# Sums of token blocks by accumulating transfers from GpSimd in an attention and feed-forward kernel

## The chip, the cores and the metric

The kernel runs on one core of one Trainium2 chip. The metric is the device time of that core in microseconds. A core has five engines, each with its own instruction queue that is worked off in order: TensorE (PE in the profile) for matrix products, VectorE (DVE), ScalarE (ACT), GpSimd (POOL) and SyncE (SP). Transfers between the chip's memory and the core's buffer are carried out by 16 DMA engines; an engine's queue only issues them. An engine stops at an instruction until everything that this instruction waits for has arrived, and all that stands behind it in the same queue stops too.

## The reference

```python
def _attn_ref(q, k, v):
    S = q.shape[2]
    scale = 1.0 / np.sqrt(q.shape[-1])
    scores = scale * np.matmul(q, k.transpose(0, 1, 3, 2)) - np.log(S)
    attn = 1.0 / (1.0 + np.exp(-scores))
    return np.matmul(attn, v)

def _moe_ref(x, w_in, w_out, s, b):
    h = x @ w_in
    r = np.maximum(h, 0.0)
    g = s * (r * r) + b
    return g @ w_out
```

q, k and v are 8 batches x 12 heads x 448 rows x 64 columns. The attention's output, laid out as 3584 tokens of 768 values, is the x of the second function; w_in is 768 x 2048 and w_out 2048 x 768. All is float32.

## The kernel before

There are two big parts. The first computes the attention, 24 pairs of head groups one after the other, and writes its output x to the chip's memory in eight pieces, one per batch (`x_dram`). Beside it VectorE and ScalarE turn the weights into the form that the second part needs.

The second part is the feed-forward network over seven blocks of 512 tokens (TB). Block 0 is done in the plain way (`ffn1`, `ffn2`). The other six are taken in two groups of three blocks, which the code calls `threes`. For a group, the 3 x 3 products of token blocks with weight blocks are not all formed: by a scheme in the manner of Strassen, 15 products of sums are formed instead, and the results are combined. Each factor is a signed sum of blocks of tokens or of weights. The sums of the weights are made once and lie in memory (`wd`); the sums of the tokens are made anew for each group, in the core's buffer. Each product is done in three matrix multiplications per tile, because every factor is split into a high and a low part (`split_hi` on ScalarE, `split_lo` on VectorE).

For each group there is a layer 1 (720 matmuls, line 1095) and a layer 2 (720 matmuls, line 1225). A layer is a loop over 60 units of 12 matmuls. `L1` gives the units' order: the 15 products in six chains, each chain for two of the four pieces p of the hidden layer at a time. The products of a chain add into the same accumulator tile (two banks of the PE's accumulators), and after each product of a chain a copy (ScalarE, `copy`, line 968) or a sum (VectorE, lines 178 and 181) takes the running sum out, before the next product of the chain may add to it. So in the chain (10, 13, 2) unit 8 is product 10 for p = 0, unit 9 product 10 for p = 1, and unit 10 is product 13 for p = 0, which goes into the tile of unit 8 and cannot begin before ScalarE has copied unit 8's result out.

The order around the change is written by hand. The nine blocks of a group, `a00` to `a22` (third of the tokens, third of the 768 columns), each 128 x 1024 float32 or 512 KB, are loaded by `load_raw`. `first_jobs(n)` makes for each of the 15 products a list of jobs: the sums of blocks that it needs (`new` for a sum into a new buffer, `into` for one into an old), then `hi` and `lo` of the split. The table `places` says after which unit u of layer 1 the next job of which product is put into the queues, and `early_jobs` does the same in layer 2 of the group before. So unit 7 has `(8,)`, and the job of product 8 that falls there is its `hi`. The job stands in ScalarE's queue ahead of the copy of unit 7's own result. Per group there are 15 sums of blocks, 30 in all, each one VectorE instruction of 128 x 1024 elements at line 178 or 181.

SyncE issues nearly all transfers: one weight fetch per unit (`wu<-wd`, line 663, 512 KB), which runs six units ahead of the PE through seven buffers; the loads of token blocks (line 337, one load in two pieces where it crosses from one batch to the next); the stores of results (line 838); and, in layer 1 of the first group only, loads and stores of `later_sums`, which makes the rest of the weight sums for layer 2 (lines 899, 902, 912). GpSimd has no work.

Of the kernel before, what the change touches and what calls it, by code (L numbers as in the profile page):

```python
# [18 lines left out]
ALU = mybir.AluOpType  # L19
# [17 lines left out]
TB = 512  # L37
# [57 lines left out]
def sigmoid_attention_relu2_ffn(  # L95
# [10 lines left out]
    nc = tc.nc  # L106
    B, NQ, P, _, _, S = qk.shape
    D = v.shape[5]
    NF, _, DM = w_in.shape
# [4 lines left out]
    KC = NCC // 3  # L114
# [8 lines left out]
    def pool(stack, name, bufs, side=None, space=None):  # L123
        kw = dict(side=side) if side else {}
        if space is not None:
            kw["space"] = space
        return stack.enter_context(
            tc.tile_pool(name=name, bufs=bufs, reuse_waits="tile", **kw)
        )
# [21 lines left out]
    heap = Slots(pool(ctx, "h0", 1), 1, "g")  # L151
# [14 lines left out]
    x_dram = [dram.tile([P, NCC, S], F32, name=f"xd_{b}") for b in range(B)]  # L166
# [59 lines left out]
    def op(o, x, sign, y):  # L226
        (add if sign > 0 else sub)(o, x, y)
# [103 lines left out]
    def load_tokens(dst, t, c0, n):  # L331

        at = t * TB
        while at < (t + 1) * TB:
            b = at // S
            m = min((t + 1) * TB, (b + 1) * S) - at
            nc.sync.dma_start(
                dst[:, :, at - t * TB : at - t * TB + m],
                x_dram[b][:, c0 : c0 + n, at - b * S : at - b * S + m],
            )  # L340
            at += m


    at = ExitStack()
# [250 lines left out]
    for n, (b, t) in enumerate(quads):  # L595
        if n:
            ticks(n, "DVE")
        a = scores(b, t, loaded[n])
# [52 lines left out]
    threes = [tuple(1 + 3 * n + i for i in range(3)) for n in range((NT - 1) // 3)]  # L651
# [14 lines left out]
    def slot(name, r=False):  # L666
        return heap.tile([P, 2, TB], F32R if r else F32, name=name)

    A = {}

    def load_raw(n, m, k):
        A[m, k] = slot(f"a_{n}_{m}{k}")
        load_tokens(A[m, k], threes[n][m], KC * k, KC)

    def split_hi(raw, sign, name):
        hi = slot(name + "h", True)
        if sign > 0:
            nc.scalar.copy(hi, raw)
        else:
            nc.scalar.activation(hi, raw, AF.Copy, scale=-1.0)  # L680
        return hi

    def split_lo(raw, sign, hi, name, own):

        lo = slot(name + "l", True)
        if sign > 0:
            sub(lo, raw, f32(hi))
        else:
            nc.vector.scalar_tensor_tensor(
                lo, raw, -1.0, f32(hi), op0=ALU.mult, op1=ALU.subtract  # L690
            )
        if own:
            heap.free(raw)
        return lo
# [3 lines left out]
    def first_jobs(n):  # L698

        jobs = {}  # L700

        def split(i, get, own=False):
            def hi():
                opd[i] = [split_hi(get(), FIRST[i][1], f"s{i}_{n}")]

            def lo():
                opd[i].append(split_lo(get(), FIRST[i][1], opd[i][0], f"s{i}_{n}", own))

            return [hi, lo]

        def a(m, k):
            return lambda: A[m, k]

        def new(key, x, y, sign=1):
            def job():
                A[key] = slot(f"a_{n}_{key}")
                op(A[key], A[x], sign, A[y])

            return job

        def into(x, y, z, sign=1, drop=()):


            def job():
                op(A[x], A[y], sign, A[z])
                for d in drop:
                    heap.free(A.pop(d))

            return job

        a00, a01, a02, a10, a11, a12, a20, a21, a22 = ((m, k) for m in range(3) for k in range(3))
        jobs[4] = split(4, a(*a00))
        jobs[3] = [new("3", a00, a20), into("3", "3", a21)] + split(3, lambda: A["3"], True)
        jobs[10] = [into(a22, a21, a22)] + split(10, a(*a22))
        jobs[13] = [new("13", a00, a22)] + split(13, lambda: A["13"], True)
        jobs[2] = [new("2", a02, a22)] + split(2, lambda: A["2"], True)
        jobs[1] = split(1, a(*a01))
        jobs[8] = [new("10", a11, a12), new("11", a01, "10")] + split(8, lambda: A["11"])
        jobs[12] = [into(a11, a10, a11), into(a11, a11, a01, 1, (a01,))] + split(12, a(*a11), True)
        jobs[7] = split(7, a(*a21))  # L740
        jobs[9] = [new("9", a10, a21, -1)] + split(9, lambda: A["9"], True)
        jobs[11] = [into(a12, a12, a21, -1, (a21,))] + split(11, a(*a12), True)
        jobs[5] = split(5, lambda: A["10"], True)
        jobs[0] = [into(a02, a02, "11", 1, ("11",)), into(a02, a02, a00, -1, (a00,))]
        jobs[0] += split(0, a(*a02), True)
        jobs[6] = split(6, a(*a10))
        jobs[14] = [into(a20, a20, a22, -1, (a22,)), into(a20, a10, a20, 1, (a10,))]
        jobs[14] += split(14, a(*a20), True)
        return jobs

# [23 lines left out]
    todo = first_jobs(0)  # L774
# [89 lines left out]
    def weights():  # L864
        fetch()
        return fetched[next(pos_)]


    places = {
# [4 lines left out]
    }  # L874
    LAST = ((0, slice(0, TB)), (1, slice(0, TB // 2)), (1, slice(TB // 2, TB)))
    LEAD = 3

# [73 lines left out]
    for n, blocks in enumerate(threes):  # L951
# [128 lines left out]
        for u, (i, p) in enumerate(L1):  # L1080
            wt = weights()
            if n == 0 and u < 4:
                load_raw(0, *start[5 + u])
            if outs and u > 4:
                out_store(outs[0], evict[6 - 2 * len(outs)], 0, 2)
                heap.free(outs.pop(0))
            ch = next(c for c in CHAINS_1 if i in c)
            if i == ch[0]:
                banks[p] = ps.tile([P, 2, TB], F32, tag="b", name=f"h_{n}_{i}_{p}")
            bk = banks[p]  # L1090
            for j in range(2):
                m = 0
                for c in range(KC):
                    for wi, xi in PARTS:
                        nc.tensor.matmul(  # L1095
                            bk[:, j], wt[:, j, wi, c * P : (c + 1) * P], opd[i][xi][:, c, :],
                            start=i == ch[0] and m == 0,
                            stop=m == 3 * KC - 1,
                            skip_group_check=True,
                        )  # L1100
                        m += 1
            if p == NPP - 1:
                for t in opd.pop(i):
                    heap.free(t)
                for key in {3: ("3",), 13: ("13",), 2: ("2",), 9: ("9",), 5: ("10",), 0: ((0, 2),),
                            12: ((1, 1),), 11: ((1, 2),), 14: ((2, 0),)}.get(i, ()):
                    A.pop(key)
            here = places.get(u, ())
            casts = []
            for q_ in (10,) * (n == 0 and u < 2) + here:  # L1110
                fn = todo[q_].pop(0)
                if u < 4 and fn.__name__ == "hi":
                    casts.append(fn)
                else:
                    fn()
            if u >= len(L1) - LEAD:
                prep(u - len(L1) + LEAD)
            ready, scales = scales, []
            for _ in range(2 - len(here)):
                if later:  # L1120
                    later.popleft()()
            results_1(i, p, bk)
            for fn in casts + ready:
                fn()
            for f, units in LATER_SUMS.items() if n == 0 else ():
                for _ in range(units.count(u)):
                    next(later_sums_[f], None)
# [10 lines left out]
        def results_2(i, bk):  # L1138
# [60 lines left out]
            elif n + 1 < len(threes):  # L1199
# [5 lines left out]
                heap.free(C.pop(4))  # L1205

        todo = first_jobs(n + 1) if n + 1 < len(threes) else {}
        loads = {38 + 2 * x: start[x] for x in range(9)} if todo else {}
        early_jobs = {50: (4,), 52: (4,), 53: (3,), 54: (3,), 55: (3,), 56: (3,), 57: (10,), 58: (10,), 59: (10,)}
        for j, (i, p) in enumerate(L2):  # L1210
            wt = weights()
            ch = next(c for c in CHAINS_2 if i in c)
# [5 lines left out]

            for e, tk in LAST if end else [(e, slice(TB)) for e in range(KC)]:
                o = bk[:, e]  # L1220
# [10 lines left out]
                if end:  # L1231
                    x = C["t"][:, e, tk]
# [57 lines left out]
```

## Time and profile before

| | |
|---|---|
| median of the runs | 1038.8 us (2 runs, 1038.2 to 1039.39) |
| span of the profiled execution, first to last instruction | 1037.5 us |
| layer 1, first group | 381.56 to 544.76 us |
| layer 2, first group | to 707.96 us |
| layer 1, second group | to 871.16 us |
| layer 2, second group | to the end |
| sums of token blocks | 1.22 us each on VectorE |

No time is given for the profiled execution as a whole; its span is 1.3 us below the median of the runs, and that is what lies around the span. The profile gives busy times per engine, a strip of 40 slices, the chain of work that ended last, groups of instructions by line and the DMA issues. The trace behind it gives each instruction's start, its length and what ended the wait ahead of it. In its rows `a<-a,a` is a sum of token blocks, `s_0h<-a` and `s_0l<-a` are the high and low part of a factor of the first group (`s_1h` of the second), `G<-h` is a copy of a result out of the accumulators, `wu<-wd` a weight fetch, and SPq is SyncE's queue as it issues transfers.

### The profile page before, as it was taken

What the parts mean: (1) busy time and instruction counts of PE and PEld (TensorE: products, weight loads), DVE (VectorE), ACT (ScalarE), POOL (GpSimd) and SP (SyncE); (2) the same over time, 40 slices, a digit from 0 to 9 for tenths busy, and PEclk for the clock granted to TensorE, in tenths of its full rate; (3) what the DMA queues carried; (4) which work ended last, traced back from release to release, by engine and by line L of the source; (5) the groups of instructions that cost most, each with busy time, mean ns of one, the idle gap of its engine ahead of it and who ended that gap; (6) DMA issues with size and microseconds to landing.
All of it is one profiled execution on the core that took longest, in us unless ns stands there. A gap on an engine that the chain in (4) does not pass through costs nothing.

```text
span 1037.5 us, 13898 instructions
## 1 busy us (share of the span) xinstructions
PE 1033.7 (100%) x5288; PEld 780.3 (75%) x5288; DVE 836.1 (81%) x906; ACT 617.2 (59%) x666; POOL 0.2 (0%) x4
## 2 busy tenths in 40 slices
PE   9999999999999999999999999999999999999998
PEld 4545555555888888888888888888888888888887
DVE  5999999995988965898898897796455789888777
ACT  7999999988776755564445344344445335552432
POOL 0000000000000000000000000000000000000000
PEclk9999999999999999999999999999999999999999
DMA  9788989995999999999686676897666666676773
GB/s 327 269 331 342 360 317 393 346 396 194 332 366 367 358 408 410 341 341 322 201 269 189 218 229 220 291 317 249 197 190 195 194 193 197 190 236 207 222 228 118
DMA packets 101568, 287.16 MB, mean 277 GB/s; under 512 B 10240, under 2 KB 20352, under 8 KB 101504
## 3 DMA queue, kind: packets, MB, share of 16 engines
q1 hardware_dynamic: 101216, 285.84, 79.6%
q8 instruction: 42, 0.69, 0.3%
q10 hardware_dynamic: 288, 0.46, 0.1%
q14 instruction: 22, 0.18, 0.0%
HBM read 198.18 MB, written 88.08 MB: 276 GB/s over the span
## 4 chain that ended last, share of the span: by engine, by line
PE 100%; DVE 0%; issue 0%
PE o L1225 31%; PE h L1095 31%; PE pav L454 11%; PE psc L420 9%; PE ph L563 6%; PE po L765 6%; PE psc_l L441 2%; PE pav L463 2%; PE psc L426 0%; PE idle L482 0%; DVE C_t L181 0%
## 5 line engine op out<-in xcount | busy, mean ns | idle before, releaser
L1095 PE MATMUL h<-s_1h,wu 128*128 128x512 f32 x480 | 148.0, 389 | 0.0
L1095 PE MATMUL h<-s_0h,wu 128*128 128x512 f32 x480 | 147.8, 389 | 0.0
L400 ACT ACTIVATE a<-psc,nls 128x896 f32<-128x896 f32 x144 | 132.7, 1008 | 12.9 <-PE psc L420 10.1
L454 PE MATMUL pav<-a,v 128*64 128x448 f32 x576 | 113.8, 543 | 0.0
L1095 PEld LDWEIGHTS h<-s_1h,wu 128*128 128x128 f32 x480 | 90.1, 188 | 18.8
L1095 PEld LDWEIGHTS h<-s_0h,wu 128*128 128x128 f32 x480 | 90.1, 188 | 18.6
L968 ACT COPY G<-h 128x1024 f32<-128x1024 f32 x48 | 48.8, 1017 | 85.5 <-PE h L1095 57.8
L860 ACT ACTIVATE G<-G,b_sb,s_sb 128x1024 f32<-128x1024 f32 x48 | 59.8, 1246 | 61.4 <-DVE G L857 60.7
L1095 PE MATMUL h<-s_0l,wu 128*128 128x512 f32 x240 | 93.4, 389 | 0.0
L1095 PE MATMUL h<-s_1l,wu 128*128 128x512 f32 x240 | 93.4, 389 | 0.0
L454 PEld LDWEIGHTS pav<-a,v 128*64 128x64 f32 x576 | 39.1, 137 | 63.8 <-issue 45.4
L178 DVE TENSOR_TENSOR G<-G,h 128x1024 f32<-128x1024 f32 x40 | 48.8, 1219 | 39.4 <-PE h L1095 39.3
L1225 PE MATMUL o<-g_3h,wu 128*128 128x512 f32 (+1 forms) x244 | 79.0, 385 | 0.0
L1225 PE MATMUL o<-g_0h,wu 128*128 128x512 f32 x240 | 78.8, 389 | 0.0
L1225 PE MATMUL o<-g_1h,wu 128*128 128x512 f32 x240 | 78.8, 389 | 0.0
L1225 PE MATMUL o<-g_2h,wu 128*128 128x512 f32 x240 | 78.8, 389 | 0.0
L765 PE MATMUL po<-g,w 128*128 128x512 f32 x288 | 67.7, 389 | 0.0
L765 PEld LDWEIGHTS po<-g,w 128*128 128x128 f32 x288 | 54.1, 188 | 11.2
L563 PE MATMUL ph<-x0h,w 128*128 128x512 f32 x192 | 61.7, 390 | 0.0
L420 PE MATMUL psc<-qkh 64*128 64x448 f32 x282 | 54.1, 380 | 0.0
L1225 PEld LDWEIGHTS o<-g_3h,wu 128*128 128x128 f32 x244 | 45.6, 188 | 9.2
L1095 PEld LDWEIGHTS h<-s_0l,wu 128*128 128x128 f32 x240 | 45.0, 188 | 9.4
(152 smaller groups left out, 2028.0 us busy)
## 6 DMA issues: line engine op xcount, KB each, us to landing
wu<-wd SPq DMA_DIRECT2D x240, 512.0 KB, 3.6
wd<-t SPq DMA_DIRECT2D x36, 768.0 KB, 8.6
qk<-qk_t SPq DMA_DIRECT2D x23, 896.0 KB, 7.4
st<-w_out SPq DMA_DIRECT2D x16, 768.0 KB, 10.3
st<-w_in SPq DMA_DIRECT2D x16, 768.0 KB, 9.3
wd<-w SPq DMA_DIRECT2D x16, 768.0 KB, 5.6
v<-v_t SPq DMA_DIRECT2D x24, 448.0 KB, 6.1
xd<-xo SPq DMA_DIRECT2D x24, 448.0 KB, 4.9
```

The lines of the kernel that those rows point to most:

```text
L178: nc.vector.tensor_tensor(o, x, y, op=ALU.add)
L400: nc.scalar.activation(a, psc[:, :, :S], AF.Sigmoid, bias=nls, scale=SCALE)
L420: nc.tensor.matmul(o[:, j, :S], two[wi][r, i, cols], two[xi][r, i, :S], start=m == 0, stop=m == 2,)
L441: nc.tensor.matmul(psc[half[i], j, :S], x[r, i, 1, 3 * P :], x[r, i, 0, :], start=True, stop=True,)
L454: nc.tensor.matmul(pav[r, i, :S], ld_[1][:, 3 * i + c, j, :], a[i, c][:, j, :], start=c == 0, stop=False,)
L463: nc.tensor.matmul(pav[r, i, :S], ld_[1][half[i], 6, j, :], a[half[i], j, :], start=False, stop=True,)
L563: nc.tensor.matmul(ph, w[:, k, wi, kc * P : (kc + 1) * P], x0[h][xi][:, cc, :], start=m == 0, stop=m == 3 * NCC - 1,)
L765: nc.tensor.matmul(pos[e], w[:, k, wi, kc * P : (kc + 1) * P], g[:, gi, :], start=first and i == 0, stop=last and i == 2,)
L860: nc.scalar.activation(x, x, AF.Identity, bias=b_sb, scale=s_sb)
L968: nc.scalar.copy(g(m, h), bk)
L1095: nc.tensor.matmul(bk[:, j], wt[:, j, wi, c * P : (c + 1) * P], opd[i][xi][:, c, :], start=i == ch[0] and m == 0, stop=m == 3 * KC - 1, sk ...
L1225: nc.tensor.matmul(o, wt[:, f, wi, e * P : (e + 1) * P], g[gi][:, f, tk], start=(end or i == ch[0] and p == 0) and f == 0 and m == 0, stop ...
```

## The change

Of the 30 sums, 14 are no longer made by VectorE. A new helper `plus` has GpSimd issue a transfer that adds its source to its destination. A sum into a new buffer becomes a plain load of one addend from `x_dram` into that buffer, issued by SyncE (`copy`), and then an accumulating transfer of the other addend (`plus_into`). A sum into an old buffer becomes the accumulating transfer alone. In each group six sums go this way (jobs `"s"`); in the second group the two sums of product 3 do too, the second of them straight from `x_dram` in two pieces (`plus_tokens`). These make 15 accumulating transfers. `SUMS_BY_DMA` places the six: two after unit 2, one each after units 4, 5, 9 and 41. The sums of product 3 in the second group are placed at step 47 of layer 2 of the first group, six steps ahead of where VectorE made them. The places of all `hi` and `lo` jobs stay as they were.

```diff
+    def plus(x, y):
+        nc.gpsimd.dma_start(out=x, in_=y, accum_op=ALU.add)
...
+        def copy(key, m, k):
+            A[key] = slot(f"a_{n}_{key}")
+            load_tokens(A[key], threes[n][m], KC * k, KC)
+
+        def plus_into(x, y, drop=()):
+            plus(A[x], A[y])
+            for d in drop:
+                heap.free(A.pop(d))
+
+        def eleven():
+            copy("11", 0, 1)
+            plus_into("11", "10")
+
+        def three():
+            copy("3", 0, 0)
+            plus_into("3", (2, 0))
+            plus_tokens(A["3"], threes[n][2], KC, KC)
+
+        def ten():
+            copy("10", 1, 1)
+            plus_into("10", (1, 2))
...
-        jobs[3] = [new("3", a00, a20), into("3", "3", a21)] + split(3, lambda: A["3"], True)
+        jobs[3] = [new("3", a00, a20), into("3", "3", a21)] if n == 0 else [three, lambda: None]
+        jobs[3] += split(3, lambda: A["3"], True)
...
-        jobs[8] = [new("10", a11, a12), new("11", a01, "10")] + split(8, lambda: A["11"])
-        jobs[12] = [into(a11, a10, a11), into(a11, a11, a01, 1, (a01,))] + split(12, a(*a11), True)
+        jobs["s"] = [
+            ten, eleven, lambda: plus_into(a11, a10), lambda: plus_into(a11, a01, (a01,)),
+            lambda: plus_into(a02, "11", ("11",)), lambda: plus_into(a20, a10, (a10,)),
+        ]
+        jobs[8] = split(8, lambda: A["11"])
+        jobs[12] = split(12, a(*a11), True)
...
-        jobs[0] = [into(a02, a02, "11", 1, ("11",)), into(a02, a02, a00, -1, (a00,))]
+        jobs[0] = [into(a02, a02, a00, -1, (a00,))]
...
-        jobs[14] = [into(a20, a20, a22, -1, (a22,)), into(a20, a10, a20, 1, (a10,))]
+        jobs[14] = [into(a20, a20, a22, -1, (a22,))]
...
+    SUMS_BY_DMA = {2: 2, 4: 1, 5: 1, 9: 1, 41: 1}
...
+            for _ in range(SUMS_BY_DMA.get(u, 0)):
+                todo["s"].pop(0)()
...
-        early_jobs = {50: (4,), 52: (4,), 53: (3,), 54: (3,), 55: (3,), 56: (3,), 57: (10,), 58: (10,), 59: (10,)}
+        early_jobs = {47: (3, 3), 50: (4,), 52: (4,), 55: (3,), 56: (3,), 57: (10,), 58: (10,), 59: (10,)}
```

The queues change at three places. The first is SyncE's queue around unit 2 of the first group. Before (`a_12` and `a_10` are token blocks, `wu_0_10_1` the weights of unit 9):

```order
L663 DMA wu_0_10_0_3855<-wd_0_91 128x1024
L337 DMA a_12_3857<-xd_85 128x2x320
L337 DMA a_12_3857<-xd_86 128x2x192
L663 DMA wu_0_10_1_3878<-wd_1_92 128x1024
L337 DMA a_10_3880<-xd_85 128x2x320
L337 DMA a_10_3880<-xd_86 128x2x192
L663 DMA wu_0_13_0_3901<-wd_0_91 128x1024
```

and in the changed kernel, where `a_10_3872` and `a_11_3876` are the new buffers "10" and "11":

```order
L337 DMA a_12_3857<-xd_85 128x2x320
L337 DMA a_12_3857<-xd_86 128x2x192
L337 DMA a_10_3872<-xd_85 128x2x320
L337 DMA a_10_3872<-xd_86 128x2x192
L337 DMA a_11_3876<-xd_84 128x2x384
L337 DMA a_11_3876<-xd_85 128x2x128
L663 DMA wu_0_10_1_3886<-wd_1_92 128x1024
L337 DMA a_10_3888<-xd_85 128x2x320
L337 DMA a_10_3888<-xd_86 128x2x192
L663 DMA wu_0_13_0_3909<-wd_0_91 128x1024
```

Four loads, together 1 MB, stand ahead of the weights of unit 9, of block `a_10` and of all that follows.

The second is GpSimd's queue, which issued nothing before. The six transfers of the first group:

```order
L672 DMA a_10_3872<-a_12_3857 128x1024
L672 DMA a_11_3876<-a_10_3872 128x1024
L672 DMA a_11_3831<-a_10_3888 128x1024
L672 DMA a_11_3831<-a_01_3807 128x1024
L672 DMA a_02_3632<-a_11_3876 128x1024
L672 DMA a_20_3551<-a_10_3888 128x1024
```

The second reads what the first writes and waits for it; the fourth adds to what the third has added to and waits for that.

The third is ScalarE's queue between units 5 and 11 of the first group, whose order is the same in both kernels. In the changed one:

```order
L1011 COPY G_003_3946<-h_4_3_3932 128x1024
L1011 COPY G_202_3963<-h_4_2_3911 128x1024
L693 CAST s_0h<-a_11_3876 128x1024
L1011 COPY G_203_3986<-h_4_3_3932 128x1024
L1011 COPY G_210_4005<-h_10_0_3990 128x1024
L1011 COPY G_211_4023<-h_10_1_4009 128x1024
```

The cast is the `hi` of product 8. Its source is now the buffer that the second accumulating transfer fills, and the copies of units 7, 8 and 9 stand behind it.

More of the change, by code (lines that the diff above doesn't have):

```diff
@@ L669, in sigmoid_attention_relu2_ffn, with plus_tokens @@
     A = {}
+    def plus(x, y):
+        nc.gpsimd.dma_start(out=x, in_=y, accum_op=ALU.add)
+    def plus_tokens(dst, t, c0, n):
+        at = t * TB
+        while at < (t + 1) * TB:
+            b = at // S
+            m = min((t + 1) * TB, (b + 1) * S) - at
+            plus(
+                dst[:, :, at - t * TB : at - t * TB + m],
+                x_dram[b][:, c0 : c0 + n, at - b * S : at - b * S + m],
+            )
+            at += m
     def load_raw(n, m, k):
```

8 rows, old and new, of the table places are left out of this document.

## The prediction

> **What bounds the kernel now.** I read the profile's first parts, then the chain of waits in order of time, and then the timelines of single queues at the places that the change touches. The page first:
>
> ```profile
> PE 1033.7 (100%) x5288; PEld 780.3 (75%) x5288; DVE 836.1 (81%) x906; ACT 617.2 (59%) x666; POOL 0.2 (0%) x4
> PEclk9999999999999999999999999999999999999999
> PE 100%; DVE 0%; issue 0%
> ```
>
> PE alone makes the chain that ends last. A busy PE in this profile need not be a PE at its pace, so the stages' lengths decide. The chain in order of time has the two groups as four pieces:
>
> ```profile
> 381.56 163.20 PE h L1095 x720
> 544.76 163.20 PE o L1225 x720
> 707.96 163.20 PE h L1095 x720
> 871.16 163.28 PE o L1225 x726
> ```
>
> All four last the same: 163.20 us / 720 = 226.7 ns per matmul, 2.72 us per unit of 12. Layer 1 of the first group, with all the extra work on VectorE and the DMA engines, is not a hundredth of a us longer than layer 1 of the second. So no matmul there waits for anything. VectorE, 81% busy, is always in time. What the change takes off VectorE can therefore gain nothing: it can only be hidden, or cost. A gain of 2% (20.8 us, about what a measurement of this kernel can tell from no change) would need fewer or faster matmuls, and the clock row is full already.
>
> **What is removed.** Fourteen sums of 1.22 us, by this group of VectorE's instructions (the larger of the two groups of such sums after 395 us):
>
> ```profile
> L178 DVE TENSOR_TENSOR a<-a,a 128x1024 f32<-128x1024 f32 x17 | 20.7, 1220 | 3.2 <-DMA a<-xd 3.1
> ```
>
> That is 14 x 1.22 = 17.1 us of VectorE's time, worth 0 by the above. The PE's work hides it, and nothing takes that cover away.
>
> **What is added.** On SyncE: five loads of 512 KB, ten issues. On GpSimd, whose queue is else empty: 15 transfers. The cost is not in issuing them. It is when a sum is ready, and who stands in a queue waiting for it. The place that has least room is product 8 of the first group. ScalarE's timeline there, before:
>
> ```profile
> 400.63 1.02 ACT L968 COPY G<-h 128x1024 f32<-128x1024 f32 x1 [1.71 <-PE h L1095]
> 401.54 1.05 ACT L678 CAST s_0h<-a 128x1024 fp32r<-128x1024 f32 x1
> 403.35 1.01 ACT L968 COPY G<-h 128x1024 f32<-128x1024 f32 x1 [0.76 <-PE h L1095]
> 406.07 1.01 ACT L968 COPY G<-h 128x1024 f32<-128x1024 f32 x1 [1.71 <-PE h L1095]
> 408.79 1.01 ACT L968 COPY G<-h 128x1024 f32<-128x1024 f32 x1 [1.71 <-PE h L1095]
> 411.75 1.06 ACT L680 ACTIVATE s_0h<-a 128x1024 fp32r<-128x1024 f32 x1 [1.42 <-DVE a L178]
> ```
>
> The copy at 400.63 is unit 6's, the cast at 401.54 is the `hi` of product 8, and the next three are the copies of units 7, 8 and 9. The PE itself needs product 8 only at unit 22, 40 us later. But the copies stand behind the cast. Unit 10 starts at 381.56 + 10 x 2.72 = 408.8 us and adds into the tile that unit 8's copy reads. From the row starts, cast and two copies take 0.95 + 0.91 + 1.01 us, with some 0.2 us to hand on: about 3.1 us. So the cast may start as late as 408.8 - 3.1 = 405.7 us, and every us beyond that stops the PE.
>
> When is the sum "11" ready? VectorE's two sums started here, held until block `a12` had landed:
>
> ```profile
> 398.81 2.49 DVE L178 TENSOR_TENSOR a<-a,a 128x1024 f32<-128x1024 f32 x2 [3.08 <-DMA a<-xd]
> ```
>
> SyncE had issued that block's two loads from 390.77 on:
>
> ```profile
> 388.94 0.33 SPq L663 DMA_DIRECT2D wu<-wd  x1
> 390.77 1.59 SPq L337 DMA_DIRECT2D a<-xd  x2
> 393.03 0.33 SPq L663 DMA_DIRECT2D wu<-wd  x1
> 393.41 1.58 SPq L337 DMA_DIRECT2D a<-xd  x2
> 395.50 0.86 SPq L663 DMA_DIRECT2D wu<-wd  x2
> 398.11 0.32 SPq L663 DMA_DIRECT2D wu<-wd  x1
> ```
>
> In the changed kernel the load for "10" comes right behind `a12`. The stretch is full of transfers:
>
> ```profile
> 392.00:403.00 11.00, 11.00 (x50) 9.09 (x50) 5.03 (x5) 5.99 (x6) 0.00 (x0) 1.00 1.05 405
> 403.00:414.00 11.00, 11.00 (x50) 9.13 (x49) 6.06 (x7) 5.56 (x6) 0.00 (x0) 1.00 1.03 415
> 414.00:425.00 11.00, 11.00 (x50) 9.09 (x49) 10.36 (x15) 6.11 (x8) 0.00 (x0) 1.00 0.82 297
> ```
>
> (last two columns: DMA share and GB/s). At some 410 GB/s 512 KB take 1.28 us, so "10" is there at 398.8 + 1.3 = 400.1, and with 0.2 us to issue the first accumulating transfer starts at 400.3. Two follow each other, each of length T from issue to landing, since the second reads what the first has written. "11" is ready at 400.3 + 2T, and the PE stops for 400.3 + 2T - 405.7 = **2T - 5.4 us**.
>
> **T is the unknown**: no row shows an accumulating transfer, or one that GpSimd issues. The nearest rows are 512 KB transfers of SyncE. A store of `t_r` between 420 and 440 us, in a gap, and the weight fetches between 380 and 420 us (min/median/max):
>
> ```profile
> wd<-t_r SPq DMA_DIRECT2D x1, 512.0 KB, 2.7
> DMA to landing us min/median/max: 4.1/7.7/9.5
> ```
>
> From below 2.7 us, the transfer nearly alone: 2T - 5.4 = 0. From above 9.5, the slowest in the full stretch: 13.6. The 7.7 of the fetches is mostly their place behind up to seven others of the same queue, which GpSimd's transfers do not have. So I build T from its parts: 2.7 - 1.28 = 1.4 us that is not moving bytes, and the bytes at half the rate, since they share the DMA engines with SyncE's, 2.6 us, or twice that if the old value of the destination must be read as well. That gives 4.0 to 6.6; I take the middle, **T = 5.3, so 5.2 us** in the first group.
>
> A rule of the Trainium skill bears on T from each side. DMA: Bandwidth & Descriptors, section "Anatomy of one DMA — SWDGE (gpsimd) path", fits a GpSimd-issued DMA as 2.0 us plus its bytes at 436 GB/s, so by an estimate from that page 3.2 us, and the stop would be 1.0 us; it is for a plain DMA, and no row here shows one. SBUF — State Buffer, section "SBUF: two separate sides", warns that GpSimd cannot write descriptors while VectorE is in a two-port mode; by it each issue would wait for up to one VectorE instruction of 1.22 us, and the stop would be 7.6 us. The same page names copies, casts and tensor-scalar operations as those in question, and the VectorE rows here are sums of two tensors, so I leave it out of the sum.
>
> **The other places.** The third and fourth transfer make the source of product 12's `hi` (at 411.75 above). The third waits for "10" in GpSimd's queue and for `a10`, which lands about 2.6 us later than before because 1 MB more stands ahead of it; it runs beside the second. The fourth lands near 400.3 + 3T = 416.2, while ScalarE, now 5.2 us late, arrives there at about 417. Nothing is added. The fifth and sixth are wanted at units 25 and 45, over 20 us later.
>
> The same place in the second group, ScalarE, then SyncE, then the landing of the token blocks between 670 and 700 us:
>
> ```profile
> 727.94 1.05 ACT L678 CAST s_1h<-a 128x1024 fp32r<-128x1024 f32 x1
> 732.47 1.01 ACT L968 COPY G<-h 128x1024 f32<-128x1024 f32 x1 [1.65 <-PE h L1095]
> 710.14 49.84 SPq L663 DMA_DIRECT2D wu<-wd  x20
> DMA to landing us min/median/max: 4.2/5.3/7.9
> ```
>
> Unit 10 starts at 735.2, the cast may start until 732.1. SyncE, which runs in step with the PE there, reaches the new loads when unit 1 ends, 707.96 + 2 x 2.72 = 713.4. Block `a12` is long there. The load needs the median 5.3 us, so with 0.2 us to issue the chain starts at 718.9 and ends at 718.9 + 2T: the stop is 2T - 13.2, below zero for T = 5.3. Cost **0**, covered by 2.6 us.
>
> Product 3 of the second group is loaded and summed from step 47 on (544.76 + 47 x 2.72 = 672.6 us), and its `hi` comes here, eight steps later:
>
> ```profile
> 670.33 0.90 SPq L337 DMA_DIRECT2D a<-xd  x2
> 698.06 1.06 ACT L680 ACTIVATE s_1h<-a 128x1024 fp32r<-128x1024 f32 x1
> ```
>
> Load 5.3 us, two transfers in sequence 2T = 10.6: ready at 672.6 + 5.3 + 10.6 = 688.5, 9.6 us early. Cost **0**.
>
> **Sum.** On the profiled execution: 1037.5 + 5.2 = 1042.7 us of span. With the 1.3 us that the runs' median lies above the span, **1044.0 us**.
>
> **The rivals.**
>
> *It is hidden altogether (0.27).* If T is at most about 3 us, the stop is under 0.6 us and the time is 1039. For it: the store at 2.7. Against it: that store ran in a gap at 420 to 440, these run at 1.05 of the DMA engines' share.
>
> *The weights come late as well (0.11).* By 425 us the change has put 1 MB of loads and five accumulating transfers more into a stretch that was full until 414: 2.6 + 5 x 1.28 = 9 us of transfer time, 15 if destinations are read too. Against it stand some 2 us that were free in 414 to 425, and the lead of the weights: those of unit 12, issued at 398.11, land by the median 7.7 us later at 405.8 and are wanted at 381.56 + 12 x 2.72 = 414.2, 8.4 us later. So 9 to 15 against 10.4 plus the stop's own 5.2: all is just covered; if the pieces do not overlap so well, up to 5 us come on top, 1049 in all.
>
> *Slower by over 2% (0.12).* The mechanism is the same wait, with a T that is several times a plain transfer's, as when the adding itself is slow or descriptors are written slowly on GpSimd. Both groups then stop at unit 10: (2T - 5.4) + (2T - 13.2). At T = 10 that is 14.6 + 6.8 = 21.4 us; from there it decides. At T = 12 it gives 18.6 + 10.8 = 29.4 us, 1068.2. Against it: no 512 KB transfer in the full stretch took more than 9.5.
>
> *Faster (0.01).* It would need a PE that waited, and the four equal stages say that it doesn't. That the sums don't move at all is ruled out by the order of GpSimd's queue.
>
> **How the numbers follow.** The forecast has 0.49: a stop of 1 to 13 us in the first group only. With T from 2.7 to 9.5 in both groups the cost runs from 0 to 13.6 + 5.8 = 19.4, that is 1038.8 to 1058.2. The range is 1038.4 to 1058.5: it holds the forecast, the hidden case and the late weights, and leaves out the slower one and a little below. Within 2%: 0.49 + 0.27 + 0.11 = 0.87; slower 0.12; faster 0.01.
>
> **What would show it.** VectorE's busy time should fall by 17 us to about 819. In the changed profile's timeline, ScalarE's cast for product 8 in the first group should wait, for a transfer and not for VectorE, until about 411, the copy of unit 8 follow at about 413, and PE be idle ahead of unit 10 only; layer 1 of the first group should last 168.4 us and the other three stages 163.2. The landing time of GpSimd's transfers gives T directly: under 3 us makes the step on the stop wrong, over 10 the whole forecast. A stop ahead of a unit that waits for `wu` would mean that the rival of the weights holds; a stop in the second group at unit 10 that T was too small.

## The result and the profile after

The changed kernel took 1062.05 us (two runs, 1059.42 and 1064.68) against 1038.8 before: a ratio of 1.0223, 95% interval 1.0203 to 1.0242. It is slower by 2.2%, 23 us, where 5 us had been forecast, and lies outside the forecast range. The execution that was profiled is the one of 1059.42 us, with a span of 1057.5, 20.0 us more than before; what follows accounts for these 20.0 us, and there is no trace of the longer run.

The page of the changed kernel, with the line of GpSimd's DMA queue:

```profile
PE 1038.2 (98%) x5288; PEld 782.8 (74%) x5288; DVE 820.1 (78%) x892; ACT 616.2 (58%) x666; POOL 14.2 (1%) x19
PEclk9999999999999997999999999999999999999999
q0 software_dynamic: 2416, 7.34, 3.6%
PE 92%; DMA 4%; issue 2%; DVE 0%; ACT 0%; POOL 0%; SPq 0%; POOLq 0%
```

VectorE has 16 us less to do, as forecast. But PE alone no longer makes the chain; transfers are in it, and the clock row has one slice at 7 tenths. Who stopped the PE, in the list of waits:

```profile
PE h L1138 <- ACT G L1011: 13.0, 2, 12.0
PE o L1270 <- DVE g_3l L181: 1.0, 1, 1.0
PE o L1270 <- ACT g_3h L693: 0.7, 1, 0.7
```

(us in total, times, longest.) The chain in order of time places these stops and gives the stages' ends:

```profile
381.10 19.05 PE h L1138 x84
409.23 8.13 DMA a<-a
...
420.31 138.51 PE h L1138 x600
558.82 130.57 PE o L1270 x576
693.36 8.12 DMA a<-a
709.64 8.29 DMA a<-xd
738.48 6.19 DMA a<-a
745.32 5.84 DMA a<-a
754.11 136.30 PE h L1138 x600
890.40 163.28 PE o L1270 x726
```

In place of three equal stages of 163.2 us there are these, from first matmul to first matmul of the next stage, for the changed kernel and the runs below:

| kernel | layer 1, first | layer 2, first | layer 1, second | time, us | ratio to before |
|---|---|---|---|---|---|
| before | 163.20 | 163.20 | 163.20 | 1038.8 | |
| changed | 177.72 | 167.01 | 164.57 | 1062.05 | 1.0223 (1.0203 to 1.0242) |
| e1_plain | 175.59 | 163.20 | 163.42 | 1051.56 | 1.0122 (1.0106 to 1.0139) |
| e2_late | 177.22 | 163.20 | 163.20 | 1055.11 | 1.0155 (1.014 to 1.017) |
| e3_second | 163.20 | 170.37 | 165.06 | 1048.68 | 1.0091 (1.0066 to 1.0116) |
| e5_block | 178.73 | 163.20 | 164.99 | 1058.84 | 1.0196 (1.0179 to 1.0213) |
| e6_spread | 171.88 | 163.20 | 163.20 | 1047.98 | 1.0087 (1.0072 to 1.0102) |
| e7_second_late | 163.20 | 163.20 | 163.20 | 1039.08 | 1.0002 (0.9993 to 1.0012) |

The stages are of the profiled execution, the times are medians, and the ratios stand with their 95% intervals. For the changed kernel the three stages are 14.5, 3.8 and 1.4 us too long, 19.7 together; with 0.45 us less ahead of them and 0.8 more behind the last stage that is the 20.0.

The first stop in detail. GpSimd's queue in the changed kernel (start, length of the issue, in brackets the idle time before it and what ended it):

```profile
400.17 1.00 POOL L672 DMA_DIRECT2D a<-a  x1 [399.73 <-PE h L1138]
409.23 1.74 POOL L672 DMA_DIRECT2D a<-a  x2 [8.06 <-DMA a<-a]
...
701.92 1.23 POOL L672 DMA_DIRECT2D a<-xd  x1 [7.71 <-DMA a<-a]
709.64 1.21 POOL L672 DMA_DIRECT2D a<-xd  x1 [6.49 <-issue]
```

The first transfer was issued at 400.17, for a forecast of 400.3, and landed at 409.23: T is 9.1 us, and the second, to 417.36, 8.1. The bracket of the first row names a matmul that ended in the same moment. In e2_late below, where that transfer has the same place, the profile names the load of its buffer, as the forecast has it (issue at 399.80). VectorE had no part in the length: it did nothing from 395.3 to 418.46 us, because its own queue stood behind ScalarE's cast. ScalarE stood with the cast of product 8:

```profile
417.38 1.04 ACT L693 CAST s_0h<-a 128x1024 fp32r<-128x1024 f32 x1 [16.19 <-DMA a<-a]
418.33 2.83 ACT L1011 COPY G<-h 128x1024 f32<-128x1024 f32 x3
```

Three copies come in a row behind it, those of units 7, 8 and 9; the second lets the PE go on with unit 10 at 420.31. And the PE goes on at half its clock. The stretches around the stop (PE busy time and count; the last columns are granted clock, DMA share, GB/s):

```profile
414.00:420.00 6.00, 0.00 (x0) 0.00 (x0) 1.54 (x2) 2.62 (x3) 0.00 (x0) 0.50 1.04 249
420.00:425.00 5.00, 4.69 (x11) 3.74 (x12) 1.31 (x3) 1.68 (x3) 2.66 (x3) 0.50 1.05 385
425.00:430.00 5.00, 5.00 (x23) 4.10 (x23) 2.85 (x3) 1.79 (x2) 0.00 (x0) 0.99 1.06 216
```

Between 420 and 425 there are 11 matmuls, between 425 and 430 there are 23. So the 12.0 us of idle time cost 14.5, and 2.5 of them are the clock. The clock fell some 3 us into the stop (the mean is 0.85 from 410 to 412 us and 0.50 from there on), and it was back about 4.8 us after the restart (0.73 from 424 to 426 us). The Trainium skill (TensorE: Matmul & The Clock Gate, section "Part 1: The HAM clock gate (the "warmup" mystery)") says that the PE's clock is at half after at least one idle window of about 3.4 us, and at full after at least one such window of sustained work. For this stop the trace agrees roughly.

At the end of layer 2 it was otherwise. There the PE stood for 0.70 us until 720.00 and for 0.96 us until 721.46, with no idle stretch of 3 us, and its clock was at half from 722 to about 725.4 us; here the measurement goes beyond what that section says:

```profile
720.00:725.00 5.00, 4.03 (x10) 2.97 (x11) 4.98 (x6) 1.04 (x1) 0.00 (x0) 0.70 0.29 107
```

### The profile page after: what moved, and what is told of

The parts are those of the page before. It is cut to its first block, busy times and chain, and to the rows that moved or that the text cites. A ratio compares the mean times of both kernels' runs of the same rounds, so it can differ in the third digit from the quotient of the medians.

```text
span 1057.5 us, 13936 instructions
## 1 busy us (share of the span) xinstructions
PE 1038.2 (98%) x5288; PEld 782.8 (74%) x5288; DVE 820.1 (78%) x892; ACT 616.2 (58%) x666; POOL 14.2 (1%) x19
## 4 chain that ended last, share of the span: by engine, by line
PE 92%; DMA 4%; issue 2%; DVE 0%; ACT 0%; POOL 0%; SPq 0%; POOLq 0%
PE h L1138 28%; PE o L1270 28%; PE pav L454 11%; PE psc L420 9%; PE ph L563 6%; PE po L807 6%; DMA a<-a 3%; PE psc_l L441 2%; PE pav L463 2%; DMA a<-xd 1%; ACT G L1011 0%; PE idle L482 0%; PE psc L426 0%; POOL a L672 0%; DVE g_3l L181 0%
## 5 line engine op out<-in xcount | busy, mean ns | idle before, releaser
L1138 PEld LDWEIGHTS h<-s_0h,wu 128*128 128x128 f32 x480 | 91.2, 190 | 31.6 <-ACT G L1011 12.4
L1270 PEld LDWEIGHTS o<-g_3h,wu 128*128 128x128 f32 x244 | 46.3, 191 | 10.6 <-ACT g_3h L693 1.1
```

The lines of the kernel that those rows point to most:

```text
L1138: nc.tensor.matmul(bk[:, j], wt[:, j, wi, c * P : (c + 1) * P], opd[i][xi][:, c, :], start=i == ch[0] and m == 0, stop=m == 3 * KC - 1, sk ...
L1270: nc.tensor.matmul(o, wt[:, f, wi, e * P : (e + 1) * P], g[gi][:, f, tk], start=(end or i == ch[0] and p == 0) and f == 0 and m == 0, stop ...
```

## The experiments

The theory to start from: the 20 us are waits in ScalarE's queue for late sums, three of them, made long by transfers of 6 to 9 us. Two questions stood against it: why a transfer takes that long, and whether the added traffic costs something by itself.

**e1_plain**: the same transfers without the adding, so this kernel leaves out the 14 sums.

```diff
-        nc.gpsimd.dma_start(out=x, in_=y, accum_op=ALU.add)
+        nc.gpsimd.dma_start(out=x, in_=y)
```

> GpSimd's 15 transfers stay where they are but copy instead of adding, so the sums themselves are left out of this kernel. Question: why does one 512 KB transfer take 8 to 9 us (first group: 400.17 to 409.23, then to 417.36 us). Theory 'the adding costs' (the old destination is read too, and the DMA engines are held longer): without it the first two transfers take 5 us or less each, the stop ahead of unit 10 shrinks from 12.0 us to 5 or less, the stop at product 3 vanishes, and the time is 1041 to 1047. Rival 'the path costs' (GpSimd writing descriptors, sharing the DMA engines with SyncE's queue): the transfers still take 7.5 us or more, and the time stays at 1055 to 1063.

Measured: 1051.56 us. GpSimd's queue and its share of the DMA engines:

```profile
400.30 0.67 POOL L672 DMA_DIRECT2D a<-a  x1 [399.85 <-PE h L1138]
407.98 1.05 POOL L672 DMA_DIRECT2D a<-a  x2 [7.02 <-DMA a<-a]
q0 software_dynamic: 2016, 7.34, 1.8%
```

The first copy took 7.7 us and the second 6.9, to 414.89. Neither side was right: the adding is worth about 1.3 us of 8.6, and the plain transfer, 7.3 us here, is the rest. The stop ahead of unit 10 is 9.3 us, as 2 x 7.3 - 5.4 = 9.2 would have it. Product 3's stop is gone too: layer 2 is at 163.20, and without the adding GpSimd issued the two pieces in one row, at 699.85. The share of the DMA engines did halve: 3.6% of 1057.5 us for 14 x 512 KB is 2.7 us of all 16 engines per accumulating transfer, against 1.35 for a copy.

**e2_late**: everything of the change stays, but the jobs that wait are placed later.

```diff
-        ... 4: (1,), 7: (8,), 8: (8,),
-        11: (12,), 12: (12, 7), 13: (7,), 14: (9,), 15: (9,), 16: (9,), 17: (11,), 18: (11,), 19: (11,),
+        ... 4: (1,),
+        12: (7,), 13: (7,), 14: (9,), 15: (9, 8), 16: (9, 8), 17: (11,), 18: (11, 12), 19: (11, 12),
...
-    SUMS_BY_DMA = {2: 2, 4: 1, 5: 1, 9: 1, 41: 1}
+    SUMS_BY_DMA = {2: 2, 4: 1, 5: 1, 17: 1, 41: 1}
...
-        early_jobs = {47: (3, 3), 50: (4,), ...
+        early_jobs = {44: (3, 3), 50: (4,), ...
```

> All transfers and sums of the change stay, but who waits for them comes later: hi and lo of product 8 from units 7 and 8 to 15 and 16, of product 12 from 11 and 12 to 18 and 19, the fifth transfer from unit 9 to 17, and product 3's sums in the second group from step 47 to 44. Theory 'the waits in ScalarE's queue are all of it': no idle PE, all four stages at 163.2 us, 1038.8 within 1.5, VectorE still some 17 us less busy than before. Rival 'the transfers crowd out the weights' (1.5 to 2.7 us of all DMA engines per accumulating transfer, five more loads): PE idle ahead of units whose weights are late, 1043 or more.

Measured: 1055.11 us. The theory holds for the second group, where both stops are gone, and falls for the first, whose layer 1 is as long as in the changed kernel. The wait in ScalarE's queue is gone there, but another had stood behind it. The PE's waits, VectorE's timeline and the weight fetches between 395 and 450 us:

```profile
PE h L1138 <- DVE G L178: 9.4, 3, 6.0
```

```profile
413.54 0.69 DVE L181 TENSOR_TENSOR t_e<-wr 128x512 f32<-128x512 f32 x1 [18.62 <-DMA wr<-wr]
418.13 2.35 DVE L178 TENSOR_TENSOR G<-G,h 128x1024 f32<-128x1024 f32 x2
```

```profile
DMA to landing us min/median/max: 6.5/11.1/17.4
```

VectorE waited for the loads of `wr` (`later_sums`; the last landed at 417.06), and the sums of units 10 and 11, which the PE needs, stood behind that work. Weight fetches, 6.9 us in the median of the same stretch before, took 11.1. Of the 14.0 us that this layer is longer, 9.4 are idle; the other 4.6 go with a granted clock of 0.69 from 414 to 425 us and 0.84 from 436 to 447. So the traffic by itself costs about as much as the first stop did. In the changed kernel no such wait shows, and the reading is that it lies hidden behind that stop. This was the rival in this expectation, only that the late transfer was not a weight fetch but a load that VectorE waits for.

**e3_second**: the change in the second group alone; the first group has the jobs and places of before.

```diff
+        if n == 0:
+            jobs[8] = [new("10", a11, a12), new("11", a01, "10")] + jobs[8]
+            jobs["s"] = []
...
+            here = (places_dve if n == 0 else places).get(u, ())
+            for _ in range(SUMS_BY_DMA.get(u, 0) if n != 0 else 0):
```

> The change in the second group alone; VectorE makes the first group's six sums as before. Theory 'three separate stops that add up': layer 1 of the first group back to 163.2 us, layer 2 of the first group still 3.7 us longer (product 3) and layer 1 of the second 1.5 us longer, 1043 to 1045 in all. Rival 'the later stops are an echo of the first' (the PE, SyncE and the transfers out of step after it): without the first stop the others vanish too, 1039 to 1040.

Measured: 1048.68 us, 1045.31 to 1050.34. The stops are separate; the later ones are no echo. That they add up to the microsecond is not shown, and 1043 to 1045 was missed: they are larger here, 9.0 us together against 5.2 in the changed kernel. Layer 2 of the first group is 7.2 us too long, with a first transfer of 10.2 us. The runs of kernels with such stops scatter by 2.4 to 5.3 us, those of the kernel before by 1.7.

**e4_alone**: nothing but transfers of 512 KB and sums on VectorE.

> Only transfers of 512 KB and sums on VectorE, nothing of the reference's computation: chains of SyncE copies, of GpSimd copies and of accumulating transfers with nothing beside them, then two and three accumulating transfers at once, a chain beside sums on VectorE, a chain beside a stream of 40 loads by SyncE, two from the chip's memory, and one block in two pieces of 64 and 448 columns. Theory 'the adding costs': alone SyncE 2.7 us, GpSimd copy 3 to 4, accumulating 5 to 6; beside loads 8 or more. Rival 'the path costs': the GpSimd copy already takes 5 us or more alone and the adding puts less than 1 us on top. Rival 'VectorE holds GpSimd up' (descriptors cannot be written while VectorE works): the chain beside VectorE's sums takes over 1 us longer per transfer than the chain alone; else the same within 0.5. The second of the two pieces is issued only when the first has landed, as in the changed kernel (701.92 and 709.64 us), if that comes from the transfers themselves.

GpSimd's queue. In a chain, the time from one row to the next is a transfer's issue, its landing and the wait:

```profile
31.90 0.56 POOL L51 DMA_DIRECT2D cp<-cp  x1 [2.60 <-DMA cp<-sy]
35.09 0.53 POOL L51 DMA_DIRECT2D cp<-cp  x1 [2.64 <-DMA cp<-cp]
43.01 0.85 POOL L35 DMA_DIRECT2D a<-a  x1 [3.92 <-DMA a<-cp]
47.91 0.86 POOL L35 DMA_DIRECT2D a<-a  x1 [4.05 <-DMA a<-a]
78.01 0.87 POOL L35 DMA_DIRECT2D a<-a  x1 [4.02 <-DMA a<-a]
82.92 0.86 POOL L35 DMA_DIRECT2D a<-a  x1 [4.04 <-DMA a<-a]
119.85 0.85 POOL L35 DMA_DIRECT2D a<-a  x1 [5.55 <-DMA a<-a]
129.97 0.86 POOL L35 DMA_DIRECT2D a<-a  x1 [9.27 <-DMA a<-a]
138.78 0.86 POOL L35 DMA_DIRECT2D a<-a  x1 [7.95 <-DMA a<-a]
198.02 1.10 POOL L35 DMA_DIRECT2D a<-src  x1 [2.18 <-issue]
```

A copy alone takes 3.2 us, an accumulating transfer alone 4.9 (43.01 to 47.91). Beside 30 VectorE sums it is 4.9 again (78.01 to 82.92), so VectorE does not hold GpSimd up. Beside SyncE's stream of loads it is 10.1 and 8.8 us (119.85 to 129.97 to 138.78). The adding is 1.7 us; beside the stream the whole takes about twice as long. The last row is the second of two pieces; GpSimd stood 2.2 us before it for nothing that the profile shows.

**e5_block**: product 3's second addend from the block in the buffer.

```diff
-            plus_tokens(A["3"], threes[n][2], KC, KC)
+            plus_into("3", (2, 1))
```

> The changed kernel with one line different: product 3's second addend comes from block a21, already in the core's buffer, as one accumulating transfer, instead of from the chip's memory in two pieces. The computation is whole. Theory 'three transfers in a row instead of two made the stop at product 3' (8.1 + 7.4 + 8.3 us): with two in a row the sum is ready 7 to 8 us earlier, layer 2 of the first group falls from 166.9 to 163.2 to 164.5 us, the other stages keep their stops, 1054 to 1060 in all. Rival 'it is the late start, or the load for the copy': layer 2 of the first group stays above 165.5 us.

Measured: 1058.84 us, and layer 2 of the first group is back at 163.20. With transfers as long as these, it was the third in the row that made the stop at product 3. ScalarE still waited 2.8 us for the sum of two, and the PE did not. The other two stops stayed, 12.4 and 1.5 us of idle PE.

**e6_spread**: e2_late with the work on the weight sums moved back by up to 4 units.

```diff
-    4: (6, 9, 9, 10, 11, 11, 11, 12, 13, 13, 14, 14),
-    5: (14, 17, 17, 18, 19, 19, 19, 20, 21, 23, 24, 24),
-    6: (22, 25, 25, 26, 27, 29, 29, 30, 31, 31, 32, 34),
+    4: (6, 13, 13, 14, 15, 15, 15, 16, 17, 17, 18, 18),
+    5: (17, 21, 21, 22, 23, 23, 23, 24, 25, 26, 27, 27),
+    6: (24, 27, 27, 28, 29, 29, 29, 30, 31, 31, 32, 34),
```

> As the run with the late places, and the making of the weight sums for f = 4, 5 and 6 in layer 1 of the first group is spread: the loads of wr stay about where they were, the VectorE and ScalarE work on them comes 3 to 4 units later. Theory 'VectorE stood at a late load of wr, with the sums that the PE needs behind it' (402.58 + 14.46 us landing, PE idle 6.0, 1.9 and 1.5 us): no or under 2 us of idle PE is left, 1039 to 1042. Rival 'the DMA engines are simply full, and the next late thing stops the PE' (weight fetches landed after 11.1 us in the median and 17.4 at most there): idle PE of 4 us or more at other places, 1045 or more.

Measured: 1047.98 us. The PE's waits now:

```profile
PE h L1138 <- DMA wu<-wd: 4.1, 1, 4.1
PE h L1138 <- DVE G L181: 1.2, 1, 1.2
```

The rival is right: with VectorE's wait out of the way, the PE stops for a weight fetch that is itself late, one that took 16.8 us. Of the 8.7 us that the layer is longer, 5.8 are idle; the rest goes with a lower clock (0.88 from 414 to 425 us). So with both placements that were tried, the six accumulating transfers cost 9 to 14 us in that stretch. Issuing them later or further apart was not tried.

**e7_second_late**: the second group alone, with the late places and product 3's addend from the block.

```diff
 (e3_second, and)
-            plus_tokens(A["3"], threes[n][2], KC, KC)
+            plus_into("3", (2, 1))
-        early_jobs = {47: (3, 3), 50: (4,), ...
+        early_jobs = {44: (3, 3), 50: (4,), ...
 (places and SUMS_BY_DMA of the second group as in e2_late)
```

> The change in the second group alone, with the late places of products 8 and 12 there, product 3's sums from step 44, and its second addend from block a21; VectorE makes the first group's six sums. Eight of the 30 sums are still made by transfers. Theory 'where the DMA engines have room, only the waits cost': no idle PE, all stages 163.2 us, the time that of the kernel before within 1 us (1037.8 to 1039.8), with VectorE 9.8 us less busy. Rival 'crowding costs there too': 1041 or more.

Measured: 1039.08 us, ratio 1.0002, interval 0.9993 to 1.0012: the same as before. The chain, and the page's row of busy times:

```profile
381.39 163.20 PE h L1153 x720
544.59 163.20 PE o L1285 x720
707.79 163.20 PE h L1153 x720
870.99 163.28 PE o L1285 x726
```

```profile
PE 1033.5 (100%) x5288; PEld 780.8 (75%) x5288; DVE 826.9 (80%) x898; ACT 616.8 (59%) x666; POOL 7.4 (1%) x12
```

A transfer takes long here too, 7.6 us for the first at each of the two places (674.19 to 681.82 and 720.40 to 727.96), but with this lead nobody waits for it. So in the second group eight of the sums can be made by transfers for nothing, and for no gain: VectorE has 9 us less to do and the PE does the same matmuls at the same pace. No version ran faster than the kernel before, and with a PE that never waits none of this kind can.

**e8_beside**: transfers again, with four times the room for GpSimd's descriptors.

```diff
-SCRATCH = 1024
+SCRATCH = 4096
```

> Only transfers of 512 KB and sums on VectorE, nothing of the reference's computation, with four times the room for GpSimd's descriptors (4096 instead of 1024 bytes): a chain of GpSimd copies beside 40 loads of SyncE, 24 loads alone, a chain of accumulating transfers beside one load per two VectorE sums (about 200 GB/s), a block in two pieces, six transfers at once. Theory 'sharing the DMA engines makes the length': the copies, 3.2 us alone, take 7 us or more beside the loads, and an accumulating one beside half the loads 6 to 7. Rival 'the sharing hits only the adding ones': the copies stay under 5. For the gap of 2.2 us between the two pieces: theory 'the room for descriptors ran out' says it is gone, the second issue follows the first within 0.2 us; rival 'a transfer from the chip's memory to the same block waits for the one before' says it stays at 2 us.

GpSimd's queue:

```profile
24.25 0.55 POOL L53 DMA_DIRECT2D cp<-cp  x1 [2.90 <-DMA cp<-a]
31.95 0.53 POOL L53 DMA_DIRECT2D cp<-cp  x1 [7.16 <-DMA cp<-cp]
39.46 0.53 POOL L53 DMA_DIRECT2D cp<-cp  x1 [6.98 <-DMA cp<-cp]
133.59 0.85 POOL L35 DMA_DIRECT2D a<-a  x1 [4.19 <-DMA a<-a]
140.08 0.84 POOL L35 DMA_DIRECT2D a<-a  x1 [5.64 <-DMA a<-a]
148.42 0.83 POOL L35 DMA_DIRECT2D a<-a  x1 [7.50 <-DMA a<-a]
178.31 2.17 POOL L35 DMA_DIRECT2D a<-src  x2 [29.06 <-DVE a L32]
```

Plain copies beside loads take 7.7 and 7.5 us: the company makes the length, adding or not. Accumulating ones beside about half the loads take 5.1, 6.5 and 8.3, where 6 to 7 had been expected; the DMA engines' share meanwhile was 0.71, 1.03 and 0.98. Six accumulating transfers at once, with nothing beside them, were done 18.0 us after the first was issued (186.44 to 204.44), 3.0 us each, near the 2.7 us of engine time. The two pieces are issued in one row, without the gap: it was the room for descriptors.

## Why the prediction was wrong, point by point

*What bounds the kernel, and that nothing can be gained*: right. e7_second_late shows it with 9 us taken off VectorE and a ratio of 1.0002.

*Where the change costs*: right for unit 10 of the first group. The start of the chain (400.17 for 400.3, in a layer that began 0.46 us sooner than before), the cast that waits, the copies behind it and the stop of 2T - 5.4 came as written: with the measured mean T of 8.6 us the formula gives 11.8, and 12.0 were measured.

*The step that failed*: "So I build T from its parts". T was 5.3 us there, and 9.1 and 8.1 on the chip. What the adding costs was about right, 0 to 2.6 us in that sum and 1.3 measured by e1_plain. Two other parts of it were off. The bytes were put at half the rate beside SyncE's transfers; e4_alone and e8_beside show a copy going from 3.2 to 7.6 us beside loads, some 4.4 us more, where half the rate would have added 1.3. And the 1.4 us "that is not moving bytes" came from a SyncE store; GpSimd's copy alone is 3.2, not 2.7. The reading of the 7.7 us of the weight fetches was the mistake behind it: I put it down to their place in SyncE's own queue and discounted it, but a transfer of another queue beside that stream took as long. The upper bound of 9.5, from the slowest row in the very stretch, was the better guide: it held for these two, and not for the third transfer, which ran beside the second and took 11.1. VectorE had no part in it: it was idle here, and beside its sums in e4_alone an accumulating transfer took the same 4.9 us. So the forecast's 5.2 us became 12.0, with 2.5 for the clock behind it.

*The third and fourth transfer, "Nothing is added"*: right in the result and not in the times. The fourth landed at 428.2 instead of 416.2, and ScalarE stood 6.5 us for it. The PE did not wait, because ScalarE's next copy came only at 431.02; the prediction had not reckoned with that, so this was luck.

*"Product 3 ... two transfers in sequence 2T = 10.6 ... Cost 0"*: failed. The sum from the chip's memory comes in two pieces, and I counted them as one. GpSimd could not issue the second until the first had landed (709.64, after 6.49 us of showing no wait), so three stood in a row, 8.6 + 7.7 + 8.3 = 24.6 us from 693.36 on. The wrong T had its part in it: three of 5.3 us would have been ready at 709.3, before the `hi` was due (558.82 + 153.3 = 712.1, by its place in layer 2 before). e5_block undoes the third transfer, and layer 2 of the first group is at 163.20; e8_beside shows that such a gap vanishes with more room for descriptors, though not in this kernel itself.

*Unit 10 of the second group, "covered by 2.6 us"*: failed by a little. From SyncE's issue at 731.72 to the first transfer it took 6.8 us instead of 5.5, and the two transfers took 6.8 and 5.8 instead of 5.3 each. That is 3.4 us more, and the PE stood 1.0 us.

*What the sum had no term for*: the clock. After the stops the PE ran at half its clock for some us. This is 2.5 of the 14.5 us in layer 1 of the first group, and about 2 of the 3.8 us in layer 2, where only 1.7 us were idle. Together, the 19.7 us are the 5.2 of the forecast, 6.8 more for T, 2.5 for the clock, 3.8 at product 3 and 1.4 at unit 10 of the second group.

*The rivals.* The hidden case fell with T. The slower one named the right mechanism, both groups stopping at unit 10, though not the cause of the long T: it gave a slow adding or a slow writing of descriptors, and it was the traffic beside. Its threshold T = 10 was too high, for want of the clock and of product 3: 2% were passed with T at 8.6. That the weights come late was given 5 us on top of the stop. In the changed kernel nothing came on top; that the PE's own stop gave the transfers time is the reading, not shown. But as e2_late and e6_spread show, the traffic costs 8.7 to 14 us of layer 1 of the first group when the stop is taken away. My account there counted an accumulating transfer as at most twice a plain one in bytes, which the 2.7 us bear out, and set against it the lead of one weight fetch; it left out the loads that VectorE waits for.

What stays open: why the second run of the changed kernel took 5.3 us longer than the one with a trace; how the DMA engines share their time, of which only the lengths were measured; and whether the first group's six sums could be made by transfers for nothing if these were issued at another time.

## What to carry to other kernels

Work taken off an engine that nobody waits for gains nothing, but what replaces it can be waited for: for each operation that is moved, ask when its result lands and what stands behind the first instruction that needs it, on that engine. Take the duration of a new transfer from at least the slowest like transfer in the same stretch, not from one that ran in a gap, and count each piece that must follow another. A stop of the PE can cost more than its length, when the clock is lower after it.

## What the runs showed of the hardware

- An accumulating transfer of 512 KB within the buffer takes 4.9 us alone, a plain one from GpSimd 3.2; both gain about 4 to 5 us beside a full stream of loads. It holds the DMA engines for 2.7 us of all 16, twice a plain one's 1.35.
- While such transfers ran, the engines were at a share of 1.04 and moved 249 GB/s (414 to 420 us of the changed kernel), where the stretches of plain ones from 392 to 414 us before had 405 and 415.
- With 1024 bytes of room, GpSimd issued the second of two accumulating transfers (64 and 448 KB of one block) only when the first had landed, 6.49 us idle in the changed kernel and 2.18 in e4_alone; the profile calls this "issue". With 4096 bytes (e8_beside), or without the adding (e1_plain), it issued both in one row.
- The PE's clock fell to half in a stop of 12.0 us, and also after two short stops of 0.70 and 0.96 us close together, but not after a single one of 1.02. In the traces' clock records each stretch at half clock within these layers is 3.4 us long or a multiple of it: 13.7 and 3.4 us in the changed kernel, 10.2 in e1_plain, 6.8 and 3.4 in e2_late.
